# FFT convolution of a 224 x 224 x 96 image: the last weight tap's rows cut into interleaved pieces, and two fillers fewer ahead of the weight matmuls

## The chip, the cores and the metric

One core of one Trainium2 chip. The metric is the device time of one execution of the program, in microseconds (us); lower is better. Engine names follow the profile: PE is TensorE's matmul and PEld its weight load, DVE is VectorE, ACT is ScalarE, POOL is GpSimd, SP is SyncE (here it only issues DMA transfers).

## What is computed

A circular convolution of an image with a 7 x 7 kernel, 96 channels in and 96 out, written with Fourier transforms over both image axes:

```python
H = W = 224; C = 96; K = 7        # x: (1, H, W, C), w: (K, K, C, C), bf16
wp = pad(w, ((0, H - K), (0, W - K), (0, 0), (0, 0)))
Xf = rfft2(x, axes=(1, 2))
Wf = rfft2(wp, axes=(0, 1))
Yf = einsum('bhwi,hwio->bhwo', Xf, Wf)
y  = irfft2(Yf, s=(H, W), axes=(1, 2)).astype(bfloat16)
```

## The kernel before, in words

The kernel transforms the height only, block by block, and does the width by its seven taps. The height is cut into eight blocks of 28 rows (each read with 6 rows of overlap); a block's transform has 17 frequencies. The width is cut into seven tiles of 32 columns, numbered t = 0 to 6. For each tile there are three stages, all of them matmuls on PE:

- the transform of the pixels, a matmul with the table `Fm`; its results go from PSUM to the tile `xf`;
- for each frequency the products with the transformed weights `WF`, over the taps of the width, on `xf` and on sums and differences of it in `J`;
- the inverse, a matmul with the table `Gm` on data that went through DRAM (`scr`, read back as `tt`), then the output's store.

The weights are transformed once. The tile `wqx` (lines 154 to 157, `wq` in the profile) holds them in 98 partitions: 49 taps times two. Partition 2k + h holds tap k's 96 x 96 matrix, flattened, from element 48h on; 9,168 elements (`WC`) of each are loaded. `PW` is 49, `PW2` 98, `C2` 48. Behind these columns lies the small table `Em`, made on the chip. A matmul reads every 96th element of all 98 partitions as its weight load (line 357), so the first one needs every column chunk of every partition. Frequencies are prepared in six groups (`PGRP`); the first group, `prep_jobs(0)`, is 48 matmuls into 12 banks, emptied into `WF` by ACT and DVE in turn.

Order of the work at the start. Instructions of one engine run in the order in which they stand. SP issues all these transfers in this order (lines 179 to 189): the halo pixels (two transfers of 112 rows and two of 6), the first half of tile 0's pixels (112 rows of 6,144 bytes and 6 rows), then the weights in five column chunks (`NWC`), each as two transfers: one of two partitions for the last tap, then one of 96 partitions for the other 48 taps:

```python
    for c0, c1 in zip(wcut, wcut[1:]):
        for k, n in ((PW - 1, 1), (0, PW - 1)):
            wdma.append(dma(wqx[2 * k:2 * (k + n), c0:c1],
```

The cuts fall at 1,792, 3,584, 5,376 and 7,296 elements. Then comes the second half of tile 0's pixels (`load_x(0, 1)`, line 188), tied by a manual dependency to the landing of the third chunk's 96 rows (`HOLD` is 2). Tile 1's pixels are issued later, behind an ACT copy of tile 0 (lines 712 to 714).

Every transfer signals its landing on one of eight semaphores, which the transfers on SP use in turn. A transfer is therefore issued only when the one eight places before it has landed, and besides when those transfers have landed whose data its own may overwrite.

PE starts with 17 filler matmuls on a zero tile `wu` (`warm(8)`, `warm(9)`, lines 195 to 200), which compute nothing that is used. Then come the transforms of tile 0's first half, 22 more fillers (lines 707 and 708), the 48 weight matmuls of `prep_jobs(0)` (line 709), the transforms of tile 0's second half (line 711), and the rounds over the frequencies with the other weight groups laid between them. In the profile all instructions bear line 89, that of the helper that keeps each engine's order; so rows are told apart by their tiles.

Of the kernel before, what the change touches and what calls it, by code (L numbers as in the profile page):

```python
# [47 lines left out]
HOLD = 2  # L48
# [8 lines left out]
def kernel(  # L57
# [7 lines left out]
    _, H, W, C = x.shape  # L65
# [5 lines left out]
    PW = KT * KT  # L71
    FR = 2 * NS
    PW2 = 2 * PW
    C2 = C // 2
    assert NJ == 8
    SYNC = mybir.DependencyInfo(mybir.DependencyClass.Sync, mybir.DependencyReason.DATA)
# [57 lines left out]
    def dma(out_ap, in_ap):  # L134
        return DE.dma_start(out=out_ap, in_=in_ap)
# [18 lines left out]
    wqx = wtmp.tile([128, C - 1 + 127 * C + 1], BF16, name="wq")  # L154
    wq = wqx[0:PW2]
    WC = C * C - C2
# [18 lines left out]
    def load_x(t, jg):  # L175
        return load_rows(xbuf(t, jg), jg, t * 2 * TW, 2 * TW)

    wsrc = w.rearrange("kh kw i o -> (kh kw) (i o)")
# [2 lines left out]
    load_x(0, 0)  # L181
    wcut = [WC * c // NWC // 128 * 128 for c in range(NWC)] + [WC]
    wdma = []
    for c0, c1 in zip(wcut, wcut[1:]):
        for k, n in ((PW - 1, 1), (0, PW - 1)):
            wdma.append(dma(wqx[2 * k:2 * (k + n), c0:c1],
                bass.AP(wsrc.tensor, wsrc.offset + k * C * C + c0, [[C * C, n], [C2, 2], [1, c1 - c0]])))
    for d in load_x(0, 1):
        tc.add_manual_dep(d.ins, wdma[2 * HOLD + 1].ins.name, SYNC, reason="second pixels behind the weights")

    wu = cpool.tile([128, 128], BF16, name="wu")
    wur = wu[:].unsqueeze(1).to_broadcast([128, 4, 128])
# [2 lines left out]
    def warm(n):  # L195
        pwu = bank()
        for _ in range(n):
            TE.matmul(pwu[:].rearrange("p (a b) -> p a b", a=4), lhsT=wu[:, 0:128], rhs=wur, start=True, stop=True)
# [505 lines left out]
    for p in range(3):  # L704
        for f in fj[p][0]:
            f()
    for n in (11, 11):
        warm(n)
    for f in prep_jobs(0):
        f()  # L710
# [159 lines left out]
    for i, (g, q) in enumerate(order):  # L870
# [3 lines left out]
        k = i + 8 - LF  # L874
        if 8 <= k < len(order):
            live[order[k]] = first(*order[k])
        if q % 2 == 1:
            w0, c0 = TL * 2 * TW + (q - 1) * 4, (q % 4 - 1) * 4 * C
# [33 lines left out]
```

## Time and profile before

| | us |
|---|---|
| median of 3 runs | 270.45 |
| lowest, highest | 270.08, 270.87 |
| the profiled execution, in all | 270.74 |
| its span, first to last instruction | 269.0 |

Of the span PE is busy 257.9 us (96%), PEld 237.1 (88%), DVE 214.3 (80%), ACT 195.5 (73%) and POOL 99.4 (37%). The chain of work that ended last is followed back from the last instruction; by engine it is PE 64%, DMA 12%, DVE 11%, ACT 7%. The mean granted TensorE clock is 0.997.

How to read the rows that follow: in a timeline row stand the start, the length, the engine, the line, the operation with output and input tiles (partitions x elements), how many, and in brackets the idle time before it and what ended it. In a row of stretches stand, after the stretch and its length, the busy time and number of instructions of PE, PEld, DVE, ACT and POOL, then the granted clock, the mean busy share of the 16 DMA engines, and the GB/s that they moved. In a row of waits stand who waited for whom, the total, how often, and the longest.

### The profile page before, as it was taken

The numbers are of one execution on the slowest core, as the hardware profiler recorded it, in microseconds if no ns is written. First come the engines' busy times: TensorE is split into PE (matmuls) and PEld (weight loads), VectorE is DVE, ScalarE is ACT, GpSimd is POOL, SyncE is SP. The second block draws the span as 40 slices with busy tenths as digits, with TensorE's granted clock in tenths as the row PEclk, the third lists the DMA queues.
The fourth block names the chain that finished last, engine by engine and source line by source line (L and its number), as shares of the span: only waits on it lengthen the run. The fifth ranks groups of instructions, "written<-read, shape, count | busy, mean of one in ns | idle before, by whom it ended". The sixth has DMA issues, their size and how long they took to land.

```text
span 269.0 us, 12171 instructions
## 1 busy us (share of the span) xinstructions
PE 257.9 (96%) x5144; PEld 237.1 (88%) x5144; DVE 214.3 (80%) x457; ACT 195.5 (73%) x483; POOL 99.4 (37%) x156
## 2 busy tenths in 40 slices
PE   8899999999999999999999999999998999899993
PEld 3679999999998999999999998989997989779862
DVE  5649998889899788778787888777887889778724
ACT  5549988587974578988988789886986864467113
POOL 7782315363647435322322222234132242522100
PEclk9999999999999999999999999999999999999998
DMA  6948011811111597987976486989658834888866
GB/s 171 230 129 217 6 46 46 243 47 67 46 46 50 163 276 135 294 249 206 289 207 198 133 246 192 250 223 332 224 151 152 255 98 154 198 231 212 223 118 205
DMA packets 47014, 46.78 MB, mean 174 GB/s; under 512 B 35286, under 2 KB 37986, under 8 KB 46960
## 3 DMA queue, kind: packets, MB, share of 16 engines
q1 hardware_dynamic: 44672, 43.94, 59.2%
q10 hardware_dynamic: 2288, 2.06, 2.8%
q8 instruction: 40, 0.66, 1.1%
q14 instruction: 14, 0.11, 0.1%
HBM read 24.65 MB, written 21.33 MB: 171 GB/s over the span
## 4 chain that ended last, share of the span: by engine, by line
PE 64%; DMA 12%; DVE 11%; ACT 7%; issue 3%; SPq 2%; DVEq 0%; ACTq 0%
PE pb L89 64%; DMA tt<-scr 5%; DMA wq<-in_w_dram 5%; DVE J L89 4%; ACT WF L89 3%; ACT xf L89 2%; DVE v L89 2%; DVE WF L89 2%; SPq L89 2%; DMA xf<-scrb 2%; DVE u L89 1%; DMA scrb<-yf 1%; DVE yf L89 1%; DVE xf L89 0%; DVE tt L89 0%
## 5 line engine op out<-in xcount | busy, mean ns | idle before, releaser
L89 PE MATMUL pb<-WF,J 96*128 96x96 bf16 x2821 | 162.6, 206 | 1.1 <-DVE J L89 0.9
L89 PEld LDWEIGHTS <-J 96*128 96x128 bf16 x2821 | 138.0, 98 | 10.5 <-issue 2.2
L89 POOL TENSOR_TENSOR yf<-v,u 128x384 bf16<-128x384 f32 x79 | 81.4, 1042 | 147.3 <-issue 86.9
L89 ACT CAST xf<-pb 96x408 bf16<-96x408 f32 (+3 forms) x145 | 67.8, 490 | 8.9 <-PE pb L89 5.3
L89 PE MATMUL pb<-WF,xf 96*128 96x96 bf16 x952 | 59.9, 206 | 0.5 <-ACT xf L89 0.5
L89 DVE TENSOR_TENSOR J<-xf 96x1824 bf16<-96x1824 bf16 (+1 forms) x84 | 56.9, 716 | 0.1
L89 PEld LDWEIGHTS <-xf 96*128 96x128 bf16 x952 | 47.0, 98 | 0.7 <-ACT xf L89 0.6
L89 PE MATMUL pb<-Fm,xn 118*128 118x136 bf16 (+3 forms) x640 | 45.5, 199 | 0.2 <-DVE u L89 0.2
L89 PE MATMUL pb<-tt,Gm 102*84 102x384 bf16 (+1 forms) x132 | 32.7, 327 | 2.4 <-DMA tt<-scr 2.3
L89 ACT CAST WF<-pb 96x480 bf16<-96x480 f32 (+1 forms) x59 | 29.1, 577 | 5.3 <-PE pb L89 5.3
L89 PEld LDWEIGHTS <-xn 118*128 118x128 bf16 x640 | 30.3, 97 | 0.3 <-issue 0.3
L89 ACT CAST J<-pb 84x384 bf16<-84x384 f32 (+1 forms) x64 | 27.6, 488 | 2.3 <-PE pb L89 2.0
L89 ACT CAST yo<-pb 84x384 bf16<-84x384 f32 (+1 forms) x63 | 26.9, 482 | 2.7 <-PE pb L89 2.7
L89 DVE TENSOR_TENSOR J<-J 96x912 bf16<-96x912 bf16 (+2 forms) x42 | 24.2, 576 | 0.0
L89 PE MATMUL pb<-wq 98*128 98x120 bf16 (+1 forms) x288 | 21.3, 226 | 0.3 <-DMA wq<-in_w_dram 0.3
L89 PEld LDWEIGHTS <-wq 98*128 98x128 bf16 x288 | 19.5, 151 | 0.8 <-issue 0.8
L89 PE MATMUL pb<-wu 128*128 128x512 bf16 (+1 forms) x75 | 16.5, 382 | 1.1 <-DVE ct L89 1.1
L89 PEld LDWEIGHTS <-wu 128*128 128x128 bf16 (+1 forms) x75 | 8.8, 119 | 7.7 <-issue 2.4
L89 DVE TENSOR_TENSOR yf<-v,u 128x384 bf16<-128x384 f32 x26 | 14.9, 571 | 0.9
L89 PEld LDWEIGHTS <-Gm 102*84 102x84 bf16 (+1 forms) x132 | 11.0, 117 | 3.5 <-DMA tt<-scr 2.9
L89 ACT COPY xf<-xf 96x816 bf16<-96x816 bf16 (+3 forms) x20 | 11.3, 632 | 0.0
L89 DVE CAST WF<-pb 96x480 bf16<-96x480 f32 (+1 forms) x13 | 7.5, 611 | 4.7 <-PE pb L89 4.7
(386 smaller groups left out, 234.4 us busy)
## 6 DMA issues: line engine op xcount, KB each, us to landing
scr<-yf SPq DMA_DIRECT2D x30, 288.0 KB
xn<-in_x_dram SPq DMA_DIRECT2D x12, 672.0 KB
tt<-scr SPq DMA_DIRECT2D x24, 336.0 KB
out_dram<-yo SPq DMA_DIRECT2D x12, 252.0 KB
out_dram<-J SPq DMA_DIRECT2D x12, 252.0 KB
tt<-scr SPq DMA_DIRECT2D x6, 288.0 KB
WF<-in_x_dram SPq DMA_DIRECT2D x2, 672.0 KB
out_dram<-tt SPq DMA_DIRECT2D x8, 168.0 KB
```

The lines of the kernel that those rows point to most:

```text
L89: r = fn(*a, **k)
```

## The change

The 96-row chunks are loaded without the last tap. The last tap's two partitions are loaded behind the second chunk, in two transfers over the whole width of 9,168 elements. Each is two partitions by eight pieces of 573 elements (1,146 bytes); the first transfer takes pieces 0, 2, 4, ..., the second pieces 1, 3, 5, .... The dependency of the second pixels is written for the new list and means the same chunk as before. The 22 fillers ahead of the weight matmuls become 20.

```diff
-    for c0, c1 in zip(wcut, wcut[1:]):
-        for k, n in ((PW - 1, 1), (0, PW - 1)):
-            wdma.append(dma(wqx[2 * k:2 * (k + n), c0:c1],
-                bass.AP(wsrc.tensor, wsrc.offset + k * C * C + c0, [[C * C, n], [C2, 2], [1, c1 - c0]])))
+    LR = PW - 1
+    wp = WC // 16
+    for c, (c0, c1) in enumerate(zip(wcut, wcut[1:])):
+        wdma.append(dma(wqx[0:2 * LR, c0:c1],
+                        bass.AP(wsrc.tensor, wsrc.offset + c0, [[C * C, LR], [C2, 2], [1, c1 - c0]])))
+        if c == 1:
+            for z in range(2):
+                dma(wqx[2 * LR:PW2, 0:WC].rearrange("p (a z b) -> p a z b", z=2, b=wp)[:, :, z],
+                    bass.AP(wsrc.tensor, wsrc.offset + LR * C * C + z * wp, [[C2, 2], [2 * wp, 8], [1, wp]]))
     for d in load_x(0, 1):
-        tc.add_manual_dep(d.ins, wdma[2 * HOLD + 1].ins.name, SYNC, reason="second pixels behind the weights")
+        tc.add_manual_dep(d.ins, wdma[HOLD].ins.name, SYNC, reason="second pixels behind the weights")
...
-    for n in (11, 11):
+    for n in (10, 10):
         warm(n)
```

In the order of the instructions, SP has three transfers fewer, PE two fillers (matmul and weight load) fewer; DVE, ACT and POOL have the same instructions in the same order. The transfers on SP now stand as: six pixel transfers, chunk 0, chunk 1, two piece transfers, chunks 2, 3 and 4, second pixels.

## The prediction

> **What bounds the kernel now.** I read the chain of work that ended last first, in order of time over the first 20 us, because the edit lies there.
>
> ```profile
> 3.40 6.14 DMA wq<-in_w_dram
> 9.53 0.02 issue
> 9.55 6.52 DMA wq<-in_w_dram
> 16.07 0.14 issue
> 16.21 0.69 PE pb L89 x8
> ```
>
> The columns are start, length, what. From 3.4 to 16.07 us the end of the kernel hangs on the weights' transfers; 0.14 us after the last landing the first weight matmul runs, and everything after it (16.21 to 269.0) is chained to it. The timeline of TensorE around this place:
>
> ```profile
> 7.64 3.49 PE L89 MATMUL pb<-Fm,WF 118*128 118x136 bf16 x103 [0.70 <-POOL WF L89]
> 10.98 4.91 PE L89 MATMUL pb<-wu 128*128 128x512 bf16 x22
> 16.21 3.15 PE L89 MATMUL pb<-wq 98*128 98x100 bf16 x48 [0.32 <-DMA wq<-in_w_dram]
> 19.20 1.10 PE L89 MATMUL pb<-Fm,WF 118*128 118x64 bf16 x32
> ```
>
> The 22 fillers end at 15.89 and PE then waits 0.32 us for the weights. So one filler is 4.91/22 = 0.223 us, and nothing useful is done on PE between 11 and 16.2: the stage is bound by the transfer engines. Their share and rate, in the last two columns of the stretches by the microsecond:
>
> ```profile
> 9.00:10.00 1.00, 1.00 (x46) 1.00 (x42) 1.00 (x3) 1.00 (x3) 0.68 (x3) 1.00 1.05 240
> 10.00:11.00 1.00, 1.00 (x41) 0.92 (x37) 1.00 (x2) 0.76 (x3) 0.73 (x4) 1.00 1.03 232
> 11.00:12.00 1.00, 1.00 (x11) 0.46 (x7) 1.00 (x3) 0.58 (x1) 0.75 (x5) 1.00 1.07 237
> 12.00:13.00 1.00, 1.00 (x7) 0.47 (x5) 0.12 (x1) 0.00 (x0) 0.74 (x4) 1.00 1.13 244
> ```
>
> They are full (share about 1) at 238 GB/s. What SP waited for between 3 and 14 us:
>
> ```profile
> SPq L89 <- DMA wq<-in_w_dram: 3.0, 2, 2.7
> SPq L89 <- DMA WF<-in_x_dram: 1.6, 2, 1.2
> ```
>
> SP has waits, but they cost nothing today: the queues on the transfer engines are still full while it waits. That cover is what the change must not lose.
>
> **What the trace records of each transfer.** The trace holds the semaphore steps of each transfer. Call the five 96-row weight transfers c0 to c4 and the two-row ones row0 to row4. Each c has 16 landings (16 engines, six pieces each), each row only two. The slower of these two engines lands c0 at 9.53, row1 9.80, c1 11.19, row2 11.50, c2 12.84, row3 13.20, c3 14.55, row4 14.77, c4 16.07: strictly in the order of issue, seven pieces in 1.65 us, 0.236 us a piece. The other engines land c4 between 13.87 and 15.54. So the five rows cost this engine 5 x 0.236 = 1.18 us, and it sets the end.
>
> **The change, part by part.**
>
> *Rows out of the five chunks.* The slow engine loses 1.18 us of work. But at best 16.07 becomes the next engine's 15.54.
>
> *Two piece transfers in.* Call them r0 and r1: two partitions, eight pieces of 1,146 bytes each, placed behind c1. How many engines carry them? The trace has no such weight transfer, but it has tt<-scr of 34 partitions x 4 pieces (136 pieces): two landings; and of 4 partitions x 12 pieces: four. The outer count decides, not the number of pieces, so r0 and r1 stay on two engines, eight pieces on each. (The Trainium skill, DMA: Bandwidth & Descriptors, section "Why a DMA increments its semaphore by 16 and not by 1", says the same: the number of engines is the largest one up to 16 that divides the slowest dimension of both sides, here two. By that rule the sixteen pieces spread nothing, and the trace's 34 x 4 transfers agree; spread over 16 engines the sum below would be 0.4 us smaller.) Eight pieces cost between 8 x 0.051 (the median of the first, 1,152-byte pieces) and, by bytes, 9,168/3,584 x 0.236 = 0.60 us; I take 0.5.
>
> *A new wait.* This is the main term. r0 and r1 interleave in the same two partitions (pieces 0, 2, 4... and 1, 3, 5...), and in the order of the changed program's instructions r1 waits for the semaphore of r0 at its second count, that is until r0 has landed. r0 stands behind c0 and c1. SP issues in order, so behind r1 stand c2, c3, c4 and the second pixels. In the old program c2 was issued at 5.73, with 5 us of work queued ahead of it; now the engines run dry. Step by step:
>
> 1. c1's landing on the slow engine was 11.19; two rows less ahead of it: -0.47; r0 itself: +0.5. r0 lands at 11.2.
> 2. SP starts 0.02 to 0.08 us after a landing (9.53 to 9.55, 12.84 to 12.92). r1's issue: two-partition issues take 0.24 to 0.59; I take 0.4, and 0.05 to the next. c2 is issued at 11.7.
> 3. From issue to first moved byte on idle engines: the next tile's pixels, issued at 20.24, first move at 21.18, 0.94 us. c2 moves from 12.65.
> 4. c2 to c4 are 96 x (3,584 + 3,840 + 3,744) = 1.07 MB; at the 238 GB/s above 4.5 us: the last byte at 17.15. Issues of 0.57 us each keep ahead of 1.4 us a chunk, and r1's pieces move in the 0.45 us before c2.
> 5. From the last c4 piece's end in the packet record, 15.11, to the landing, 16.07, are 0.96 us. The weights have landed at 18.1.
> 6. 0.14 us later, as now, PE starts: 18.25 against 16.21: **+2.04 us**.
>
> Bounds of this sum: the rate is the unknown. At the 313 GB/s of 15 to 16 us (6 KB pieces) step 4 takes 3.4 us and the sum is +0.95; at the 215 GB/s of the second of the next tile's two pixel loads (0.69 MB from landing to landing, 3.2 us) 5.0 us, +2.55. I keep 238, measured on these very transfers. With r0 0.3 us earlier or later the whole is about +0.7 to +2.8.
>
> *Two fillers fewer.* -0.45 us of PE: the fillers end at 15.44. They are off the path as soon as the weights come later, so they save nothing; they lengthen PE's idle stretch to 18.25 - 15.44 = 2.8 us.
>
> *Second pixels* (tile 0's other half). They still wait for c2, so their issue moves from 12.92 to about 15.3, while c4 is still queued. They now end about 2 us behind c4 (17.1 against 15.1) and land at 18.26; after the change about 20.3. They are needed after the weight matmuls (19.20 now, 21.24 then): the slack stays 0.9 us, cost nothing. If the second pixels were 1 us later still, PE would wait for them.
>
> *Five issues to two and fewer PE instructions* on SP: nothing, SP is waiting anyway. Nothing else moves: order and counts on ACT, DVE and POOL are the same.
>
> *Does +2.04 reach the end?* Behind 16.21 PE idles 0.46 us once before 43 us, for ACT work that follows from the weights, and the chain then is 64% PE. The next tile's pixels are issued behind ACT work that shifts too. I pass it on in full. Against the profiled execution (269.0 span, 270.74 in all) this gives 272.8; the median of the runs, 270.45, is 0.29 below that execution, so **272.5**.
>
> **Rivals.**
>
> *The clock falls in the gap.* The stretches at the kernel's end:
>
> ```profile
> 264.75:267.45 2.70, 0.01 (x1) 0.00 (x0) 0.58 (x2) 0.58 (x2) 0.00 (x0) 1.00 0.83 258
> 267.45:269.00 1.55, 0.00 (x0) 0.00 (x0) 0.00 (x0) 0.00 (x0) 0.00 (x0) 0.50 0.02 8
> ```
>
> The granted clock (third number from the end) went to 0.50 only 2.70 us after the last matmul, while 0.7 us of idle at 7 us did not do it. My gap of 2.8 us lies at this edge. (The Trainium skill, TensorE: Matmul & The Clock Gate, section "Part 1: The HAM clock gate", lets the clock fall after an idle window of about 3.4 us; by it 2.8 us would be safe and the forecast stands. The trace's 2.70 us speaks against such comfort.) The first full clock came 3.57 us after the first matmul (1.05 to 4.63), so half clock may hold for some 3.4 us, part of it in the gap. The 48 weight matmuls, 3.15 us, and what follows would lose up to half of 3.4 us, 1.7; ACT and DVE, which empty these banks in about 3 us, hide some: +0.9 to +1.7, I take +1.3: 273.8. It may strike some runs only.
>
> *The engines refill fast, or r0 is early.* With 313 GB/s and r0 landing at 10.9, the sum is about +0.7: 271.1, within 0.3% (0.81 us, about what a measurement of this kernel can tell from no change). Against it: the rate of these pieces was 232 to 244 in four stretches.
>
> *No gap at all: not slower.* If r0's pieces pass c0 and c1 on their engines, r1 could go early. The point from which it decides: r0 landed by about 8.2, so that c2's first bytes (1.45 us later) come before the engines run dry at about 9.7 (10.69, c1's last landing on the other engines, less 0.96). Then c4 lands near 15.6 to 15.9, the shorter fillers are the cover, and PE starts 0.3 to 0.5 us earlier: 270.1. Against it: the landing ladder above, in the order of issue everywhere.
>
> *The pieces spread over 16 engines after all* (the change then does what it says): r0 adds one piece per engine and lands at 10.8, the sum is +1.6: 272.1, inside the forecast's range.
>
> **How the numbers follow.** Gap without clock loss, spread or not: 0.52 (271.3 to 273.2). Gap with clock loss: 0.33 (272.5 to 274.7). Fast refill: 0.08. No gap: 0.04. Still slower for a reason not seen (second pixels late): 0.03. Likeliest: 272.5. The range, 271.2 to 274.2, leaves out the fast cases and the top of the clock case. Slower by over 0.3%: 0.52 + 0.33 + 0.03 = 0.88; within: 0.08; faster: 0.04.
>
> **What would show it.** In the changed profile: SP idle from about 4.8 to 11.2 for a weights transfer; transfer share near 0 for 2 to 3 us around 10 to 12.6; first weight matmul near 18.25, with PE idle 2.8 us before it, released by the weights; fillers ending at 15.44; the granted clock either 1.00 throughout (forecast) or 0.50 for a stretch near 17 to 22 us. I am wrong if c2 is issued before 10, or the first weight matmul starts before 17.

## The result, and the profile after

| | before | after |
|---|---|---|
| median of 6 runs, us | 270.54 | 274.49 |
| lowest, highest | 270.08, 270.87 | 273.76, 275.83 |
| the profiled execution, in all | 270.74 | 274.59 |
| its span | 269.0 | 272.9 |

The ratio is 1.0149, with a 95% interval of 1.0126 to 1.0172: slower by 4.0 us. The forecast was 272.5 and its range ended at 274.2; the direction was right, the time is above the range. The ratios, here and below, leave out single executions more than 1.5% above the fastest of their kernel, which the medians include: 274.43 in run 2, 1435.5 in run 3, 363.83 in run 4, 277.34 in run 5, 276.17 in run 11, and two of the kernel before (273.98, 273.55).

The chain of work that ended last, in order of time (start, length, what), in the changed kernel:

```profile
4.48 6.10 DMA wq<-in_w_dram
10.59 0.02 issue
10.60 0.25 SPq L89
10.85 0.04 issue
10.90 0.57 SPq L89
...
12.51 5.51 DMA wq<-in_w_dram
18.01 0.35 issue
18.36 5.00 PE pb L89 x72
```

The first piece transfer is issued at 4.48 and lands at 10.59; only then does SP issue the second (10.60) and chunk 2 (10.90). SP's own waits between 3 and 14 us are one row, and the transfer engines' share and rate (the last two columns of the stretches) fall while it lasts:

```profile
SPq L89 <- DMA wq<-in_w_dram: 5.6, 1, 5.6
```

```profile
9.00:10.00 1.00, 1.00 (x41) 0.98 (x38) 1.00 (x3) 1.00 (x4) 0.68 (x3) 1.00 0.26 61
10.00:11.00 1.00, 0.95 (x35) 0.87 (x33) 1.00 (x2) 0.62 (x2) 0.74 (x4) 1.00 0.12 25
11.00:12.00 1.00, 1.00 (x10) 0.45 (x7) 1.00 (x3) 0.58 (x1) 0.75 (x5) 1.00 0.07 16
```

In the same three microseconds they moved 240, 232 and 237 GB/s before. PE's timeline:

```profile
10.97 4.48 PE L89 MATMUL pb<-wu 128*128 128x512 bf16 x20
18.36 3.72 PE L89 MATMUL pb<-wq 98*128 98x100 bf16 x48 [2.92 <-DMA wq<-in_w_dram]
21.89 1.70 PE L89 MATMUL pb<-Fm,WF 118*128 118x64 bf16 x32
```

The fillers end at 15.45, PE waits 2.92 us, and the weight matmuls start 2.15 us later than before. But then they also run longer: 3.72 us for 3.15, and 1.70 for 1.10 behind them. The stretches tell why (the third number from the end is the granted clock):

```profile
18.00:19.70 1.70, 1.33 (x22) 1.37 (x23) 0.88 (x2) 0.64 (x2) 1.44 (x5) 1.00 0.66 199
19.80:23.20 3.40, 3.40 (x53) 3.40 (x52) 2.52 (x6) 2.68 (x6) 0.88 (x3) 0.50 0.00 0
```

For 3.4 us PE runs at half clock, all of it behind the gap. The first `scr` store, in the kernel before and in the changed one:

```profile
33.05 0.36 SPq L89 DMA_DIRECT2D scr<-yf  x1
36.31 0.36 SPq L89 DMA_DIRECT2D scr<-yf  x1
```

It is 3.26 us late: 2.15 from the late weights and 1.11 more. The last output stores are 3.84 us late; the 0.6 between them comes up after 90 us.

### The profile page after: what moved, and what is told of

It is laid out like the page before. It is cut to its first block, busy times and chain, and to the rows that moved or that the text cites. A ratio compares the mean times of both kernels' runs of the same rounds, so it can differ in the third digit from the quotient of the medians.

```text
span 272.9 us, 12165 instructions
## 1 busy us (share of the span) xinstructions
PE 259.2 (95%) x5142; PEld 238.3 (87%) x5142; DVE 214.5 (79%) x457; ACT 195.6 (72%) x483; POOL 98.4 (36%) x156
## 4 chain that ended last, share of the span: by engine, by line
PE 61%; DVE 14%; DMA 11%; ACT 5%; issue 5%; SPq 3%; POOL 0%; ACTq 0%; DVEq 0%
PE pb L89 61%; DVE J L89 5%; DMA tt<-scr 5%; DMA wq<-in_w_dram 4%; DVE WF L89 3%; DVE v L89 3%; SPq L89 3%; ACT WF L89 2%; DVE u L89 2%; DMA xf<-scrb 1%; ACT xf L89 1%; DMA scrb<-yf 1%; DVE yf L89 1%; DVE xf L89 1%; POOL yf L89 0%
```

## The experiments

The first theory: the wait of the second piece transfer for the first delays the weights by about 2.1 us, the idle PE loses its clock, and that costs 1.1 us more. The rivals: the pieces themselves are slow, the two missing fillers do it, or the clock has no part. Two marks tell the terms apart in each trace: the start of the weight matmuls (16.21 before) and the first `scr` store (33.05). Where the store is later by more than the start, something between them was lost.

**1. More fillers under the wait.** `for n in (10, 10)` becomes `(16, 16)` in the changed kernel.

> The changed kernel with 32 fillers in place of 20 ahead of the weight matmuls, nothing else. The fillers end at about 10.97 + 32 x 0.224 = 18.1 us, just under the weights' landing at 18.0. Theory (the wait between the two piece transfers costs 2.1 us, and the idle stretch of 2.9 us on PE lowers the clock, which costs 1.1 us and more): first weight matmul unchanged at about 18.4, granted clock 1.00 from 10 to 30 us, 272.7 in all (270.5 + 2.15), range 272.4 to 273.0. Rival (the clock's fall is no cause, all of the 3.9 us follows from the late weights): 274.3 as before the edit.

Measured: 274.12 median, ratio 1.0150 (1.0119 to 1.0180). In the profiled execution (273.3) the clock stays at 1.00, and the lateness no longer grows: weight matmuls +2.81, first store +2.77.

```profile
19.02 3.14 PE L89 MATMUL pb<-wq 98*128 98x100 bf16 x48 [0.99 <-DMA wq<-in_w_dram]
```

By this mark the extra 1.1 us are the clock's. The median does not show it: it lies at the rival's 274.3. In the profiled execution the weights landed at 18.58, not at 18.0, and the later start took over half of what the clock gave. Of the six executions, three at a mean clock of 0.996 to 0.998 took 273.3 to 273.6 us, three at 0.990 to 0.994 took 274.6 to 275.4.

**2. The same bytes without interleaving.** In the changed kernel the pieces are cut as a left and a right half:

```diff
-dma(wqx[2 * LR:PW2, 0:WC].rearrange("p (a z b) -> p a z b", z=2, b=wp)[:, :, z],
+dma(wqx[2 * LR:PW2, 0:WC].rearrange("p (z a b) -> p z a b", z=2, b=wp)[:, z],
-    ... + z * wp, [[C2, 2], [2 * wp, 8], [1, wp]]))
+    ... + z * 8 * wp, [[C2, 2], [wp, 8], [1, wp]]))
```

> The changed kernel with the two piece transfers as the left and the right half of the columns, which do not interleave, at the same place in the queue and with the same bytes; 20 fillers. Each half is then one run of 9,168 bytes per partition. Theory (the wait of the second piece transfer for the landing of the first is the cause): no SP wait at 4.9 us, chunk 2 issued before 6, weights landed at 15.8 to 16.2, first weight matmul at 15.9 to 16.3, clock 1.00, 270.2 to 270.8 in all. Rival (two transfers over the whole width on two engines are slow by themselves, or 20 fillers are too few): first weight matmul later than 17, or the clock at 0.50, and above 271.5.

Measured: 270.36, ratio 0.9993 (0.9973 to 1.0013), no change against the kernel before. PE does not wait at all, with the 20 fillers of the change:

```profile
10.96 4.48 PE L89 MATMUL pb<-wu 128*128 128x512 bf16 x20
15.51 3.15 PE L89 MATMUL pb<-wq 98*128 98x100 bf16 x48
```

The weights landed at 15.15. The whole loss is gone with the overlap of the two transfers, though they still go over the whole width and on two engines. The halves are not cut into small pieces any more (the trace has four packets of 9,168 bytes in place of 32 of 1,146), so this run does not clear the pieces; runs 6 and 7 do.

**3. The fillers alone.** `(11, 11)` becomes `(10, 10)` in the kernel before.

> The kernel before with 20 fillers in place of 22, nothing else. Theory (fillers matter only through PE's idle stretch, which is 0.8 us here): same start of the weight matmuls at 16.2, clock 1.00, 270.2 to 270.8. Rival (two fillers fewer are enough to lose the clock): a stretch at 0.50 between 16 and 24 us and 271.5 or more.

Measured: 270.76, ratio 1.0030 (1.0002 to 1.0057). Most executions are like those of before, but four of twelve took 271.6 to 273.1 us. The profiled one (272.15) is of these: one engine landed its last chunk at 17.16 (the others by 15.10), PE idled 1.51 us, and the clock fell. (The row names a transfer of pixels as what ended the wait; the second pixels landed only at 18.96, the weights 0.14 us before the start.)

```profile
17.30 3.66 PE L89 MATMUL pb<-wq 98*128 98x100 bf16 x48 [1.51 <-DMA WF<-in_x_dram]
```

```profile
19.00:22.30 3.30, 3.30 (x53) 3.30 (x52) 2.49 (x5) 2.48 (x7) 1.52 (x4) 0.50 0.02 5
```

Here the rival was partly right. A gap of 1.5 us was enough here, and two fillers fewer are two fewer against a late landing. The weight matmuls are 1.09 us late, the store 2.13: the clock again costs 1.04.

**4. The rows on twelve engines.** Four transfers of one partition, twelve pieces of 764 bytes each, even pieces ahead of chunk 0, odd ones behind chunk 4:

```diff
+    wp = WC // 24
+    def tap(z):
+        for h in range(2):
+            dma(wqx[2 * LR + h:2 * LR + h + 1, 0:WC].rearrange("p (a z b) -> p a z b", z=2, b=wp)[:, :, z],
+                bass.AP(wsrc.tensor, wsrc.offset + LR * C * C + h * C2 + z * wp, [[C2, 1], [2 * wp, 12], [1, wp]]))
+    tap(0)
...
+    tap(1)
```

> The last tap's two partitions in four transfers of one partition each, twelve pieces of 382 elements (764 bytes), even and odd pieces apart; the two even ones ahead of chunk 0, the two odd ones behind chunk 4, so that the even ones have long landed when the odd ones are issued; 20 fillers. Theory (the number of engines follows the outer count, here 12, and the two engines with the rows set the end of the weights): twelve landings for each, no SP wait for a weights transfer before chunk 3, the weights landed at 15.3 to 15.7, first weight matmul at 15.5 to 15.8, 269.7 to 270.2 in all. Rival (one partition means one engine whatever the pieces): one landing each, weights at 16.0 or later, 270.5 or more.

Measured: 270.93, ratio 1.0016 (0.9995 to 1.0038). Each of the four has twelve landings, so the outer count does set the engines; the weights have landed at 15.23 and their matmuls start at 15.47, 0.74 us earlier. The total misses the expectation: the first store is only 0.33 us earlier, and nothing of it is seen at the end. Run 9 follows that.

**5. Fillers past every landing.** `(19, 19)` in the changed kernel.

> The changed kernel with 38 fillers, nothing else: they end at about 10.97 + 38 x 0.223 = 19.4 us, past any landing of the weights seen so far (18.0 and 18.6). Theory (beyond the late weights the changed kernel pays for the clock, and with 32 fillers a late landing still left a gap in some runs): PE does not wait for the weights, first weight matmul at 19.5 (+3.3), granted clock 1.00 from 10 us to the end, and the runs lie close together, 273.2 to 274.2, though the weight matmuls start 1.1 us later than in the changed kernel. Rival (the spread up to 275.4 comes from somewhere later in the kernel): single runs above 274.8 remain, or the median is over 274.8.

Measured: 274.69, ratio 1.0144 (1.0105 to 1.0184), runs from 272.6 to 277.3. At the start the theory held: no wait, clock 1.00, weight matmuls at 19.36 (+3.15), first store +3.12, nearly as late as the changed kernel's +3.26. Fillers that cover the gap cost about what the clock would. The runs did not lie close together, and the median is above the expected range. Three at a mean clock of 0.998 to 1.000 took 272.6 to 273.7 us, the other three more than 275.6. The profiled one is the slowest (277.3) and shows the clock falling much later, after PE waited 3.02 us for `tt`:

```profile
236.76 0.86 PE L89 MATMUL pb<-tt,Gm 102*84 102x384 bf16 x2 [3.02 <-DMA tt<-scr]
```

```profile
235.80:242.60 6.80, 5.84 (x55) 4.97 (x56) 1.15 (x3) 2.97 (x7) 1.98 (x2) 0.50 0.82 196
```

So the rival named a true source of scatter.

**6. The change's own pieces, with no chunk behind the wait.** The first piece transfer goes ahead of chunk 0, the second behind chunk 4 (`tap(z)` issues piece transfer z as the change does):

```diff
+    tap(0)
     for c, (c0, c1) in enumerate(zip(wcut, wcut[1:])):
...
+    tap(1)
```

> The changed kernel with its own two interleaved piece transfers and 20 fillers, but the first ahead of chunk 0 and the second behind chunk 4: the first has long landed when the second is issued, so the wait finds nothing to wait for, and no chunk stands behind it. Theory (the wait and what stands behind it are the whole cause): no idle stretch of the transfer engines, weights landed at 15.2 to 16.0, first weight matmul 15.5 to 16.2, 269.9 to 270.7 in all. Rival (eight pieces on each of two engines, or interleaved writes, are slow): first weight matmul after 17 and above 271.5.

Measured: 271.15, ratio 1.0042 (1.0022 to 1.0063). The wait itself did not go: the first piece transfer landed at 8.86, and SP stood 2.2 us for it before it issued the second at 8.94. By then all five chunks were issued. The weight matmuls start at 16.71, 1.65 us earlier than in the changed kernel and 0.50 later than before:

```profile
16.71 3.15 PE L89 MATMUL pb<-wq 98*128 98x100 bf16 x48 [1.27 <-DMA wq<-in_w_dram]
```

Chunk 4 landed at 15.42, the second piece transfer at 16.36. The pieces behind the last chunk end the weights 0.94 us later than the chunk does, and my expectation left that out. It is 0.5 us at the weight matmuls and at the first store; the median is 0.94 above that of before. So the pieces cost little, and what costs is a wait with chunks behind it. PE's 1.27 us of idle did not lower the clock.

**7. The wait alone, put into the kernel before.** All ten transfers and 22 fillers stay:

```diff
+            if len(wdma) == 5:
+                tc.add_manual_dep(wdma[4].ins, wdma[3].ins.name, SYNC, reason="third chunk behind the second")
```

> The kernel before, all ten weight transfers and 22 fillers as they were, with one wait added: the two-row transfer of the third chunk is issued only when the second chunk's 96 rows have landed (11.2). Theory (such a wait empties the transfer engines for 2 to 3 us whatever the pieces are): transfer share near 0 for about 2 us after 10 us, weights landed at 18.2 to 18.8, first weight matmul 18.3 to 18.9 after 2.4 to 3.0 us of PE idle, the clock at 0.50 for one window of 3.4 us, 273.6 to 275.2 in all. Rival (the cost is in the pieces): 271.5 or less.

Measured: 274.27, ratio 1.0146 (1.0123 to 1.0169): the change's whole loss, without any of its pieces and with all 22 fillers.

```profile
10.00:11.00 1.00, 1.00 (x47) 1.00 (x44) 1.00 (x2) 1.00 (x4) 0.75 (x4) 1.00 0.03 8
11.00:12.00 1.00, 1.00 (x25) 0.68 (x22) 1.00 (x3) 0.69 (x3) 0.75 (x5) 1.00 0.10 24
...
20.00:23.30 3.30, 3.30 (x53) 3.30 (x52) 2.49 (x5) 2.51 (x6) 0.68 (x2) 0.50 0.05 16
```

SP's wait is 5.3 us here. The transfer engines empty at the same time, the weight matmuls start at 18.42 (+2.21), the clock falls for 3.4 us, and the first store is 3.20 us late.

**8. Halves with 22 fillers.** Run 2 with `(11, 11)`.

> The last tap as a left and a right half as in the run with halves, but with 22 fillers. Theory (with halves the weights land at 15.2 to 16.0 and the fillers set the start): first weight matmul at about 15.95, no idle stretch, clock 1.00 in all, runs 270.0 to 270.9. Against the run with halves and 20 fillers (median 270.36): 0.2 to 0.5 us slower by the later start, or equal if its early start is given back later, where its scr stores were only 0.31 us earlier than in the kernel before. Rival (20 fillers leave gaps that cost clock): 22 fillers are faster by 0.3 us or more.

Measured: 270.25, ratio 0.9996 (0.9978 to 1.0014). The weight matmuls start at 15.69, the first store is 0.33 us earlier, as with 20 fillers: equal, by the expectation's second half.

**9. Where the early start is given back.** In run 2, ACT's row for the sine of the table `Gm` says:

```profile
20.82 0.37 ACT L89 ACTIVATE ct<-ct,ct 102x84 f32<-102x84 f32 x1 [0.84 <-POOL ct L89]
```

POOL's chain is done at 20.8 here, as in the kernel before (20.89), though the weights came 0.7 us earlier. Edit: run 2 with one instruction instead of two in its three floor divisions.

```diff
-            GE.tensor_single_scalar(out=out_ap, in_=out_ap, scalar=MAGIC, op=ALU.add)
-            GE.tensor_single_scalar(out=out_ap, in_=out_ap, scalar=MAGIC, op=ALU.subtract)
+            GE.tensor_scalar(out=out_ap, in0=out_ap, scalar1=MAGIC, scalar2=MAGIC, op0=ALU.add, op1=ALU.subtract)
```

> The last tap as a left and a right half, 20 fillers, and the POOL chain that makes the table Gm three instructions shorter: in its three floor divisions, adding and subtracting the rounding constant are one instruction instead of two. In the run with halves the weight matmuls started 0.70 us earlier than in the kernel before, but the scr stores only 0.31 us, because ACT's copy of this chain (the sine for Gm) still waited until 20.8 for POOL, 0.84 us. POOL's ops of this chain take 0.45 (84 columns, one of the three) and 0.25 to 0.4 us (one column, two of the three): the chain ends about 1.0 us earlier, at 19.8. Theory (ACT stands in order behind POOL's chain and gives the early start back there): ACT waits 0.2 us or less for POOL, the first scr store 0.6 to 0.8 us earlier than in the kernel before, 269.3 to 270.1 in all. Rival (the gain is lost elsewhere): scr stores 0.3 us early as without the edit, 270.0 to 270.6.

```profile
20.01 0.37 ACT L89 ACTIVATE ct<-ct,ct 102x84 f32<-102x84 f32 x1
```

ACT's wait is gone, and the early start (15.66, -0.55) now reaches the first store in full (-0.59). The total does not show it and misses the expectation: 270.46, ratio 1.0000 (0.9987 to 1.0014).

**10. The shorter POOL chain alone, in the kernel before.**

> The kernel before with the shorter POOL chain alone. There ACT waits 0.19 us for this chain, and what follows on ACT waits for PE anyway. Theory (the weights' landing at 16.1 sets the pace there): scr stores within 0.2 us of the kernel before, 270.0 to 270.7. Rival (the POOL chain bounds the kernel before as well): 0.5 us faster or more.

Measured: 270.06, ratio 1.0004 (0.9979 to 1.0029). In its profiled execution the weights landed 0.45 us early, at 15.62, and the store is 0.5 us early with them; the runs show no gain. No version tried here beats the kernel before by more than the runs scatter; those without the wait beat the changed one by about 4 us.

**11. The clock alone.** The kernel before with `(6, 6)` fillers: early weights and an idle PE.

> The kernel before with 12 fillers in place of 22, transfers untouched: the fillers end at about 13.65 and the weights land at 15.6 to 16.1 as before, so that only PE's idle stretch grows, to 2.0 to 2.6 us. Theory (idle stretches of 1.5, 1.9 and 2.0 us within one window of the clock lowered it in three runs, 1.0 and 1.3 us did not in two; a lowered clock behind the gap costs 1.0 to 1.1 us by the first scr store): first weight matmul at 15.8 to 16.3, clock 0.50 for 3.4 us from somewhere between 14.5 and 20 us, first scr store 0.7 to 1.3 us later than it would be by the start of the weight matmuls (33.05 at a start of 16.21), 270.9 to 271.9 in all. Rival (the clock's fall needs late weights or a longer gap): clock 1.00, first scr store at the start of the weight matmuls + 16.8 us, 270.0 to 270.7.

Measured: 273.32, ratio 1.0123 (1.0071 to 1.0175), more than expected. In the profiled execution (272.24) the weights came early and the clock fell:

```profile
15.40 3.95 PE L89 MATMUL pb<-wq 98*128 98x100 bf16 x48 [1.66 <-DMA wq<-in_w_dram]
```

```profile
16.20:19.50 3.30, 3.30 (x45) 3.30 (x44) 2.58 (x6) 2.70 (x6) 2.84 (x8) 0.50 0.02 6
```

The weight matmuls start 0.81 us early, the first store is 0.12 us late: 0.93 us lost between (run 2 gave back 0.4 of such an early start to POOL, so the clock's own share lies between 0.5 and 0.9). An idle PE with punctual weights costs time by itself. The mean clock of the six runs lies between 0.98 and 1.00, and the two at 0.98 took 276 us. But the one at 1.000 took 271.96, 1.6 us above the median of before, so not all of this run's loss is the clock's; what else it is stays open.

**12 to 15. Where the scatter comes from.** Three more executions of the changed kernel (12, 13, 15) and one of run 11's (14), each with its trace.

> The changed kernel again, one look with its trace, to see in which stretch the time beyond +3.3 us at the first scr store goes. Theory A (a second fall of the clock, behind PE's wait for tt or scra data between 195 and 265 us): an execution of 274.8 us or more shows clock 0.50 there, one below 274.4 shows none, and the wait before such a fall is 1.3 us or longer. Theory B (the fall at 16 to 20 us lasts two windows in some executions): clock 0.50 for 6.8 us there and the first scr store 4 us or more later than before. Theory C (only waits, no clock): slow executions with clock 1.00 after 24 us.

> The changed kernel, a second look; theories A, B and C as in the first.

> The kernel before with 12 fillers, one look with its trace: its executions lay between 271.9 and 276.2 though the first scr store of the profiled one was only 0.1 us late. Theory A: an execution above 273.5 shows the clock at 0.50 after 195 us. Theory B: two windows of 0.50 at 14 to 24 us. Theory C: clock 1.00 after 24 us.

> The changed kernel, a third look; theories A, B and C as in the first.

They took 272.98, 273.89, 272.89 and 274.62 us; one run of the kernel before beside them took 271.73. Run 15 is the case of two stretches of 3.4 us at half clock:

```profile
18.00:21.00 3.00, 2.27 (x28) 2.30 (x29) 1.52 (x3) 1.04 (x3) 2.41 (x7) 0.50 0.47 129
21.00:24.00 3.00, 3.00 (x47) 3.00 (x46) 2.09 (x5) 2.39 (x5) 0.00 (x0) 0.50 0.02 5
```

By execution, in us against the kernel before:

| | weight matmuls | first store | between | clock at 0.50 | last stores |
|---|---|---|---|---|---|
| changed, first profile | +2.15 | +3.26 | 1.11 | 3.4 | +3.84 |
| changed, run 12 | +1.95 | +2.87 | 0.92 | 3.4 | +2.20 |
| changed, run 13 | +1.98 | +2.81 | 0.83 | 3.4 | +3.03 |
| changed, run 15 | +2.52 | +4.11 | 1.59 | 6.8 | +3.82 |

So theory B is seen in one execution; it ended no later than the first profile, whose clock fell for one window only. What lies behind the first store moves the end by -0.7 to +0.6 us: a part in waits for `tt` and for `scra` (the last tile's part of what goes through DRAM), which differ from execution to execution. Run 14 is theory C: it waited 2.53 us for `tt` at 202.9 without a fall of the clock, and its last stores are 2.33 us late though its first store is only 0.21 late. Theory A is shown in two other runs only (5 and 8, near 234 us). No trace exists of the changed kernel's two executions of 275 to 276 us, but their mean clock is on record: 0.985 and 0.981, against 0.991 to 0.993 in the four below. By (1 - clock) x span / 0.5 that is some 8 and 10 us at half clock against 4 to 5, so a second or a longer fall belongs to them (an estimate; the idle end of the kernel, 0.5 to 2.5 us in the four traces, is part of each figure). Whether A or B stays open.

## Why the prediction was wrong, step by step

**What bounds the kernel, and the new wait: right.** +2.04 was predicted, +1.95 to +2.52 came in four executions. That it came so close is partly luck, for single terms erred and cancelled: r0 landed at 10.59, not 11.2 (c1 on the slower engine gained more than two rows); r1's issue took 0.25, not 0.4; chunk 2 was issued at 10.90, not 11.7. But the refill took longer: from chunk 2's issue to the last landing 7.1 us, where I had 6.4. PE started 0.35 us after the landing, not 0.14. Run 2 takes the wait away, run 6 what stands behind it, and run 7 puts it in alone.

**Two engines for sixteen pieces: right.** Two landings for each piece transfer, twelve in run 4. (This is the rule of the Trainium skill, DMA: Bandwidth & Descriptors, section "Why a DMA increments its semaphore by 16 and not by 1"; both traces agree.)

**"They save nothing", of the fillers: right in the changed kernel, but not the whole of it.** Run 3 shows that two fillers are part of the cover against a late landing.

**"My gap of 2.8 us lies at this edge": the step that failed.** The idle stretch was as forecast (2.92). I took the 2.70 us between the last matmul and the fall at the kernel's end for the shortest idle time that lowers the clock, gave the fall a chance of 0.33, and forecast the time without it. The 2.70 us are only one idle time that does. The record of the clock, read whole, says more: its stretches between changes are 262.826, 249.173, 13.653, 6.827 and 3.413 us, all multiples of 3.413. So the clock changes on a fixed grid in each execution, and the idle time inside one window of this grid sorts the cases at the weight matmuls:

| run | PE idle in one window, us | clock fell |
|---|---|---|
| 1 | 0.99 | no |
| 6 | 1.27 | no |
| 12 (16.73 to 20.14) | 1.43 | yes |
| 3 | 1.51 | yes |
| 11 | 1.66 | yes |
| 14 | 1.82 | yes |
| 7 | 1.85 | yes |
| changed, first profile | 1.98 | yes |
| 15 | 2.39 | yes |
| 13 | 2.75 | yes |

About 1.4 us were enough at the weights, less than half of a window. Later in the kernel the line is less sharp: 1.61 us in run 8 and 2.05 in run 5, both near 234 us, lowered the clock; 1.50 in run 14 (204 to 207 us) did not, nor did 1.41, 1.42, 1.45 and 1.66 in one of the last windows of runs 7, 4, 8 and 14. Why these differ is not known. In every whole window of these traces with 1.82 us or more the clock fell. A gap of 2.8 us leaves at least 1.4 us in one of the two windows that it can straddle, and in about three quarters of the positions of the grid 1.82 or more. So the chance was at least 0.75 (an estimate from these windows), not 0.33. The fall came in all four traces of the changed kernel. (The Trainium skill, TensorE: Matmul & The Clock Gate, section "Part 1: The HAM clock gate", gives the window, 3,413 ns and free-running, and this case agrees with that to the nanosecond. That an idle window is needed does not fit these traces: windows with more than half of their time busy lowered the clock.)

**The price of the fall: right in size.** I had +0.9 to +1.7 and took +1.3; 0.83 to 1.11 for one window, 1.59 for two. A second window came where the first one after the fall still began with idle time (0.89 us in run 15, 0.98 in run 5); in the falls of one window it held 0.17 us or less. I had not thought of that.

**"I pass it on in full": right on the mean, with scatter.** The second pixels landed at 20.52 and were needed at 21.89, 1.4 us of slack for the 0.9 forecast. A shift the other way is not passed on in full: 0.4 us of an earlier start ends in ACT's wait for POOL (runs 2 and 9).

The sum of the two terms as predicted, 2.04 + 1.3, gives 273.8; the measured 274.49 is 0.7 above, the size of the later scatter, which no run pins to one cause. The forecast chose the wrong one of its two cases. The time lies in the range that the prediction gave for the other, 272.5 to 274.7, of which the forecast's range left out the top.

## What to carry to other kernels

Two transfers that interleave in the same partitions can count as overlapping: look in the order of instructions for a transfer that waits for the one before it, and ask how long the queue behind it lasts. Here waits of the issuing engine cost nothing while the queue was full (4.6 us in the kernel before, between 3 and 14 us); the 5.6 us that let it run empty cost 2.15 us at the weights. Where PE must idle, count the idle time inside one window of its clock, from the record's own grid, before taking a gap for harmless.

## What the runs showed of the hardware that was not expected

The clock fell with only 1.43 us idle in a window of 3.413 us, and stayed at half for a second window where the first at half clock began with 0.89 or 0.98 us of idle. Eight 1,146-byte pieces on each of two engines, behind the last chunk, landed 0.94 us after it, where I had reckoned 0.4 to 0.6. The same issue differed in length between executions: chunk 3's took 0.95 us in the first profile of the changed kernel, 0.60 to 0.64 in the three later ones, 0.57 before.
